# Last stage loaded at once, the last step's rows in one output product, Wo requested earlier, column-tiled softmax sums, and a new instruction order

## Chip, cores, metric

One core of a Trainium2 chip. The metric is the device time of one execution in microseconds (us); a kernel is judged by the median of its runs, and kernels are compared only with runs on the same chip. The time before was 1850.33 us, the median of 3 runs (1847.67 to 1852.43).

## The reference, cut to what matters

```python
def _A_ref(x, mem0, Wq, Wk, Wv, Wo, seg_len):        # x 1x2048x512, 32 heads of 128, segments of 32 rows
    mem = mem0                                       # 8 memory rows
    for s in range(n_seg):                           # 64 steps, one after the other
        h = concat([mem, x[segment s]])              # 40 rows
        q, k, v = h @ Wq, h @ Wk, h @ Wv
        p = softmax(where(mask, q @ k.T * scale, -1e9))
        o = (p @ v) @ Wo
        mem = o[:, :8]                               # the next step needs it
        outs.append(o[:, 8:])

def _B_ref(x, wqkv, wo):                             # linear attention, 32 heads of 16
    pq, pk = phi(q), phi(k)
    num = pq @ (pk.T @ v); den = pq @ sum(pk) + 1e-6
    return (num / den) @ wo

x = x + _A_ref(_layernorm(x), ...)                   # "layer 1"
x = x + _B_ref(_layernorm(x), ...)
x = x + _A_ref(_layernorm(x), ...)                   # "layer 2"
x = x + _B_ref(_layernorm(x), ...)                   # its output part is "the last stage"
```

Everything is bf16 at the interface. Only the memory rows tie a step to the one before; what depends on x alone (the "left" part: 32 queries and keys of a group of four steps for the first 8 rows of each segment) can be done ahead.

## The kernel before

The kernel records every operation with its reads, writes and an estimated cost, and a list scheduler puts them in one order per engine. A table OFFSET holds, for each kind of operation, how much earlier or later than its step it should be taken; the numbers were found by tuning. The parts that matter:

```python
# softmax sums of the x rows: ones-block matrix times the exponentials, in the full array
def sums(pe):
    o = tl.f32()[:, 256:512].rearrange("p (h q) -> p h q", h=8)
    pe.matmul(o, bo_sb[:, :], Px[:, :, :], start=True, stop=False)
    return pe.matmul(o[:, :, 0:8], bo_sb[:, :], PLL[:, g2, :, gl], start=False, stop=True)
# ... cut: projections, scores and output product run as four column tiles of 128x32 (tile_position=(0, 32 * j))

# scores of the left block, two halves; the keys and queries come from DMA transposes (step > 0)
turned(Wq_sb, "Wq", blk, bk, b, qTl[:, r2, hs, :, :], ("qTl", r2, b), False, step > 0)
turned(Wk_sb, "Wk", blk, bk, b, kTl[:, r2, hs, :, :], ("kTl", r2, b), False, step > 0)
at(step, "lefts")
for b in range(2):
    ...
    add("pe", mm, c_pe4(16, 32), reads=[("kTl", r2, b), ("qTl", r2, b)], tiles=[tl], mode="col")

# residual of a group: after the fourth step the left rows get an output product of their own
if g == 3:
    u = out_proj(oTl[:, :, :], [[("oTl", b)] for b in range(2)], False)
    add("pe", lambda pe: pick(pe, lambda d: sell_sb[:, d, :], u, False, True), ...)

# last stage: tile t in one of four buffer sets
(x, xk), (e, ek, rb, rk) = LAST[t % len(LAST)]
x_move(x, xs_view[t], ...); x_move(e, pq_view[t], ...)      # reload from DRAM
add("pe", md, ...)                                           # denominators into td
add("act", ... Ln ...); add("act", ... Exp scale=-1 ...)     # rb = 1 / den
add("dve", ... e = e * rb ...)
for c in range(4): add("pe", ... ty += e[:, c].T @ MB[c] ...)
add("dve", ... x = x + ty ...); x_move(o_view[t], x, ...)    # store
```

The softmax here doesn't subtract the row's maximum and nothing guards it: scores larger than these inputs give would overflow.

Of the kernel before, what the change touches and what calls it, by code (L numbers as in the profile page):

```python
# [19 lines left out]
MODE_SLACK = 13.61  # L20

LOOK = 0.082
# [3 lines left out]
    "ld0": (0.70,),  # L26
    "ld1": (-0.40,),
    "ld2": (2.30,),
    "ld3": (5.55,),
    "ld4": (8.15,),  # L30
    "startF": (-0.35,),
    "prepF": (4.00, -2.60, -0.45, 1.15, -4.65, 7.00, 14.55, -3.50, 0.90, -3.80, -3.10),
    "left0F": (-4.40, 2.85, 0.60, 32.60, -4.25, 0.00, 32.50, 0.00),
    "left1F": (0.05, -2.15, -4.10, 4.75, 3.10, 18.25, 7.20, 1.95),
    "leftv0F": (-3.10, -1.85),
    "leftv1F": (-1.40, -10.40),
    "leftsF": (-0.95, -0.75, 2.95, 0.45),
    "xlF": (-1.65,),
    "qk0F": (-10.50, -0.55, -0.25, 20.50, -0.40, -1.35, 3.25, -1.35),
    "qk1F": (-1.00, -1.60, 4.65, -4.45, -11.35, -1.55, 12.75, 1.30),  # L40
    "v0F": (7.00, 9.60),
    "v1F": (20.55, -10.50),
    "mem0F": (1.05, 7.85, -0.55, -5.55, -17.00, -0.80, -0.25, 0.65, 8.20),
    "mem1F": (2.70, -2.55, -1.85, 3.15, -3.55, -7.15, -0.35, -24.55, -0.75),
    "outF": (-1.20, 10.05, 1.30, 0.10),
    "nextF": (3.80, -27.25, 1.30),
    "xF": (3.05, -0.25, -1.40, 27.60, -0.70, -1.90, -2.30, -5.85, 1.30, 6.10, 1.25, 6.15, 2.10, -6.95, -10.55,
        -32.90, 1.90, 17.30, 22.35, 15.65, 14.45, 7.40, 2.20),
    "qk0": (-6.65, -8.45, 2.80, -2.85, 0.75, -1.95),
    "qk1": (0.10, 0.50, -3.40, 6.60, 0.30, 7.35, 4.45, 0.00),  # L50
    "v0": (-0.35, -1.85),
    "v1": (1.10, -1.15),
    "mem0": (-7.20, 3.30, -4.60, -15.00, -14.10, -29.60, -1.10, -8.65, 1.10),
    "mem1": (4.95, 4.35, 2.30, -3.40, 0.85, 0.30, -0.30, 0.55, -0.20),
    "out": (-5.75, 3.60, 2.10, 0.00),
    "next": (-2.35, -2.70, 4.60),
    "res": (46.85, 9.10, -4.95, 0.45, -2.55, -2.35, 3.70),
    "x": (-2.40, 4.35, 3.50, 2.50, -2.75, -1.05, 18.10, -12.50, 0.00, 2.95, -11.30, -1.85, -2.60, -8.75, 1.05,
        5.10, 2.15, 20.75, -0.75, -2.90, 22.45, 15.20, -6.80),
    "prep": (-2.95, 9.15, 2.55, 3.15, 5.35, 1.20, 8.00, 14.55, -3.30, -1.15, 2.05),  # L60
    "left0": (1.40, 1.75, -0.55, -3.10, 2.35, -0.10),
    "left1": (-1.30, -12.85, 2.90, 28.00, -8.10, 0.90),
    "leftv0": (33.85, -3.25),
    "leftv1": (8.30, -8.25),
    "lefts": (-13.05, 27.25, 3.50, 0.05),
    "xl": (3.95,),
    "bi": (3.50, 0.15, 0.85, 0.85, -1.40, -9.55, 1.30, -7.60, -0.40, -5.70, 7.90, 3.90, 15.75, -3.20, 9.80,
        -8.55, -3.95, 1.25, 19.45, -0.25, -5.15, -10.65, -5.50),
    "xL": (17.05, 17.65, -5.75, 4.55, 0.00, -4.45, -1.50, -0.10, -4.55, -3.55, -4.45, 2.55, 0.80, 6.30, -5.95,
        4.25, 6.20, -9.30, -0.65, 6.15, 11.35, -14.35, 0.00),  # L70
    "outL": (0.00, 4.55, 2.10, -7.75),
    "resL": (1.90, 17.60, -4.15, -8.15, -4.70, -0.80, 10.70),
    "biL": (0.00, 5.25, -8.20, 1.20, 5.75, 0.00, 6.85, 7.75, -3.55, 6.55, -0.45, 0.50, 0.40, 3.70, 10.65,
        -25.10, 17.00, -4.45, 1.45, -4.25, 10.90, -1.45, -0.20),
    "bm": (14.50, -2.55, -2.20, -1.25, -15.85, -11.15, -10.00, 0.00, -4.45, 11.90, 32.55, 2.50, -11.35),
    "boF": (-4.80, -11.80, 5.50, 2.35, -12.80, -4.45, -19.45, -9.45),
    "bo": (-31.10, 6.35, -4.05, 10.85, 22.70, 6.80, -2.55, -1.15),
    "boL": (2.25, 5.05, -6.15, 20.80, 7.70, -12.90, -0.15, -3.00, -9.15),
# [407 lines left out]
def _build_kernel(nc, A_x, A_mem0, A_Wq, A_Wk, A_Wv, A_Wo, A_seg_len, B_wqkv, B_wo, out):  # L486
# [6 lines left out]
    assert D == 512 and H == 32 and DH == 128 and M == 8 and SEG == 32 and S % 128 == 0  # L493
# [35 lines left out]
    sell_sb = sb("sell_sb", [128, 2, 128], F32R)  # L529
    outW = sb("outW_sb", [128, 3, 256], F32R)  # L530
# [44 lines left out]

    SCR = [("kTl", 1, 0), ("kTl", 1, 1)]
    scr_flat = kTl[:, 1, :, :, :].rearrange("p h j x -> p (h j x)")
    A8_sb = scr_flat[:, 0:128]
    scr_sb = scr_flat[:, 128:848]
    MEM0 = ("vl", 1, 0)  # L580
    mem0_sb = vleft[:, 1, 0:512]

# [10 lines left out]
    XV = ["xlnT", "vB"]  # L593

# [37 lines left out]
    for i, (W, v, nm, t) in enumerate(((Wq_sb, qk_view[0], "Wq", 12.4), (Wk_sb, qk_view[1], "Wk", 22.0),  # L632
                                       (Wv_sb, qk_view[2], "Wv", 31.0))):
        P.at(-9000 + 1000 * i, "ld%d" % (2 + i))
        late.append(add("act", lambda a, W=W, v=v: a.dma_start(W[:, :, :], v), 0.5, writes=[nm], dsem="d" + nm, lat=t))
    wo_view = A_Wo.rearrange("h e d -> e h d")
    P.at()
    for i in range(4):
        hs = slice(8 * i, 8 * i + 8)
        nd = add("sp", lambda s, hs=hs: s.dma_start(Wo_sb[:, hs, :], wo_view[:, hs, :]), 0.9, writes=[("Wo", i)],  # L640
                 dsem="dWo%d" % i, after=[late[-2]], lat=(12.4, 5.6, 5.7, 5.8)[i])
        late.append(nd)
    add("sp", lambda s: s.dma_start(wqkv_sb[:, :, :], B_wqkv.rearrange("(c p) f -> p c f", p=128)), 0.5,
        writes=["wqkv"], dsem="dwqkv", after=[late[-1]], lat=5.0)
# [38 lines left out]
    for j in range(4):  # L683
        q = slice(32 * j, 32 * j + 32)
        d = j % 2

        sel(scr_sb[q, 8 * d:8 * d + 8], ALU.not_equal, 1.0, 0, [[-1, 8]], 1, *SCR)

        o = 16 + 224 * d + 96
        sel(scr_sb[q, o:o + 24], ALU.not_equal, 1.0, -8, [[-1, 24]], 1, *SCR)  # L690

        for g4 in range(4):
            o = 464 + 128 * d + 32 * g4 + 24
            sel(scr_sb[q, o:o + 8], ALU.not_equal, 1.0, -8 * g4, [[-1, 8]], 1, *SCR)
# [5 lines left out]
    pool(lambda g: g.memset(A8_sb[:, :], 1.0), SCR)  # L700
    sel(A8_sb[0:8, :], GE, 0.0, 0, [[1, 128]], -16, *SCR)
    sel(A8_sb[0:8, :], GE, 0.0, 15, [[-1, 128]], 16, *SCR)
# [3 lines left out]
        reads=SCR, tiles=[tl])  # L706
# [40 lines left out]
    cnt = {"m": 0}  # L747

    def a_layer(base, first):
        def at(s, name):  # L750

            P.at(base + s, name + ("F" if s <= 0 else "L" if s >= NSEG or (s == NSEG - 1 and name == "x") else ""))
# [134 lines left out]
        def x_attention(s):  # L887
# [25 lines left out]
            def sums(pe):  # L913
                o = tl.f32()[:, 256:512].rearrange("p (h q) -> p h q", h=8)
                pe.matmul(o, bo_sb[:, :], Px[:, :, :], start=True, stop=False)
                return pe.matmul(o[:, :, 0:8], bo_sb[:, :], PLL[:, g2, :, gl], start=False, stop=True)
            add("pe", sums, c_pe(1, 256) + c_pe(1, 64), reads=["Px", ("PLL", g2), "bo"], tiles=[tl])
# [11 lines left out]
            for b in range(2):  # L929
# [13 lines left out]
                pvv = lambda pv=pv: pv.f32()[:, :].rearrange("p (n q) -> p n q", q=32)  # L943
                evac(oTb[:, s1, 16 * b:16 * b + 16, 8:32], lambda pvv=pvv: pvv()[:, :, 8:32], 384, tiles=[pv],
# [52 lines left out]

        def residual(G, g, w):
# [6 lines left out]
            def pick(pe, sel, u, first, last):  # L1005
                for d in range(2):
                    r = pe.matmul(tl.f32()[:, 256 * d:256 * d + 256], sel(d), outW[:, u, :], start=first and d == 0, stop=last,  # L1007
                                  skip_group_check=True)
                return r
            add("pe", lambda pe: pick(pe, lambda d: selx_sb[:, d, 96 - 32 * g:224 - 32 * g], w, g == 0, False),  # L1010
                0.42, reads=[("outW", w, 0), ("outW", w, 1), "selx"], tiles=[tl])
            if g == 3:
                u = out_proj(oTl[:, :, :], [[("oTl", b)] for b in range(2)], False)
                add("pe", lambda pe: pick(pe, lambda d: sell_sb[:, d, :], u, False, True),
                    0.42, reads=[("outW", u, 0), ("outW", u, 1), "sell"], tiles=[tl])
# [30 lines left out]
        for s in range(NSEG):  # L1046
# [6 lines left out]
            for b in range(2):  # L1053
                at(s, "qk%d" % b)
                hs = slice(4 * b, 4 * b + 4)
                turned(Wq_sb, "Wq", blk, bk, b, qT[:, r2, hs, :, :], ("qT", r2, b), True, QDMA[b] and s > 0)
                turned(Wk_sb, "Wk", blk, bk, b, kT[:, r2, hs, :, :], ("kT", r2, b), True, KDMA[b] and s > 0)
# [16 lines left out]
            if g == 2 and G + 1 < NT:  # L1074
                prepare(G + 1, s)
        w = out_block(NSEG)
# [74 lines left out]
    def b_mid(step, n):  # L1151
# [9 lines left out]
        for c in range(4):  # L1161
# [9 lines left out]
    LAST = [((x_sb[:, 0, :], ("x", 0)), OWN),  # L1171
            ((x_sb[:, 1, :], ("x", 1)),
             (half(qT[:, 0], 0), [("qT", 0, 0)], whole(kT[:, 0]), [("kT", 0, 0), ("kT", 0, 1)])),
            ((x_sb[:, 2, :], ("x", 2)),
             (half(qT[:, 0], 1), [("qT", 0, 1)], vimg[:, 0, :].bitcast(F32), [("v", 0, 0), ("v", 0, 1)])),
            ((vleft[:, 0, 0:512], ("vl", 0, 0)), LEFT)]

    def b_out(step, t, last):

        P.at(step, "boL" if last else "bo" if t else "boF")  # L1180
        k = t % len(LAST) if last else slot(t)
# [83 lines left out]
```

## Time and profile before

| | before |
|---|---|
| time, median | 1850.33 us |
| TensorE busy | 1760 us, 95% |
| start to the first next-memory product | 54.98 us |
| steps of both layers (62 between the first and last of 63 marks, twice), without the end of layer 1 | 1670.8 us |
| end of layer 1 (last next-memory product to the first of layer 2) | 58.05 us |
| last next-memory product of layer 2 to the first multiply of the last stage | 33.4 us |
| first multiply to last addition of the last stage | 30.5 us |

The marks are the starts of the last matmul that picks the next memory rows (L988 before, L1012 after) in a step, and of VectorE's first and last operation of the last stage.

### The profile page before, as it was taken

Reading aid. Unit: us, or ns where it says so; the run is one execution under the profiler, and the core shown is the slowest. Engines: PE = TensorE matmul, PEld = TensorE weight load, DVE = VectorE, ACT = ScalarE, POOL = GpSimd, SP = SyncE. Lnnn points to the kernel's source line nnn. Section 1 sums busy time; section 2 is a strip of 40 time slices with the busy share of each in tenths; the row PEclk is TensorE's granted clock in tenths of the full one; section 3 lists DMA queues with packets and bytes.
Section 4 is the critical chain, followed back from the end, with each engine's and each line's share of the span. In section 5 each row is a group of like instructions: output and inputs, shape, how many; then the busy total and the mean of one; then the engine's idle time right before and its main releaser. Section 6 shows DMA issues by size and latency. Waiting matters only on the chain.

```text
span 1850.0 us, 99018 instructions
## 1 busy us (share of the span) xinstructions
PE 1760.3 (95%) x45752; PEld 1181.3 (64%) x45861; DVE 1041.4 (56%) x3161; ACT 1207.3 (65%) x3133; POOL 74.7 (4%) x172
## 2 busy tenths in 40 slices
PE   5899999999999999999799999999999999999996
PEld 2566666666666666676456666666666676666662
DVE  3365555555555555555555555565655656555555
ACT  3566666666666676666466667666666766666655
POOL 3000000000000000000000000000000000000000
PEclk9999999999999999999899999999999999999998
DMA  9322222212121221222012122222221212223214
GB/s 358 92 42 38 39 40 36 45 38 46 37 42 37 38 44 40 43 38 40 22 26 40 38 46 41 46 43 38 43 41 38 49 40 43 41 41 55 43 34 125
DMA packets 221743, 95.53 MB, mean 52 GB/s; under 512 B 205096, under 2 KB 215472, under 8 KB 219792
## 3 DMA queue, kind: packets, MB, share of 16 engines
q1 hardware_dynamic: 214128, 61.01, 17.7%
q0 software_dynamic: 5616, 15.60, 3.0%
q10 hardware_dynamic: 1584, 12.58, 1.7%
q8 instruction: 358, 5.87, 1.3%
q14 instruction: 57, 0.47, 0.1%
HBM read 29.89 MB, written 10.49 MB: 22 GB/s over the span
## 4 chain that ended last, share of the span: by engine, by line
PE 84%; DMA 11%; ACT 2%; DVE 2%; issue 1%; ACTq 0%; SPq 0%; DVEq 0%
PE pb L764 38%; PE pb L963 16%; DMA arena_sb<-arena_sb 9%; PE pb L939 4%; PE pb L848 4%; PE pb L786 3%; PE pb L1007 3%; PE pb L865 2%; PE pb L1102 2%; PE pb L903 2%; ACT arena_sb L602 2%; PE pb L1138 1%; PE pb L879 1%; DMA Wk_sb<-in_A_Wk_dram 1%; PE pb L878 1%
## 5 line engine op out<-in xcount | busy, mean ns | idle before, releaser
L602 ACT ACTIVATE arena_sb<-pb 128x512 bf16<-128x512 f32 (+6 forms) x1369 | 704.7, 525 | 337.9 <-PE pb L764 269.7
L764 PE MATMUL pb<-Wk_sb,arena_sb 128*32 128x512 bf16 x5120 | 345.4, 381 | 4.8 <-DMA Wk_sb<-in_A_Wk_dram 4.6
L764 PE MATMUL pb<-Wq_sb,arena_sb 128*32 128x512 bf16 x5120 | 342.9, 383 | 4.7 <-DMA Wq_sb<-in_A_Wq_dram 0.6
L764 PE MATMUL pb<-Wv_sb,arena_sb 128*32 128x512 bf16 x5120 | 345.1, 379 | 0.3 <-issue 0.3
L963 PE MATMUL pb<-Wo_sb,arena_sb 128*32 128x256 bf16 x10368 | 324.2, 275 | 5.4 <-issue 3.0
L603 DVE CAST arena_sb<-pb 128x128 bf16<-128x128 f32 (+3 forms) x411 | 161.9, 394 | 246.0 <-PE pb L988 152.3
L963 PEld LDWEIGHTS pb<-Wo_sb,arena_sb 128*32 128x32 bf16 x10368 | 266.5, 97 | 28.2 <-DVE arena_sb L882 13.4
L924 DVE TENSOR_TENSOR arena_sb<-arena_sb 32x256 bf16<-32x256 bf16 x512 | 213.4, 417 | 108.1 <-ACT arena_sb L920 95.5
L603 DVE COPY arena_sb<-pb 128x512 bf16<-128x512 bf16 (+2 forms) x318 | 124.2, 391 | 175.0 <-PE pb L786 164.5
L764 PEld LDWEIGHTS pb<-Wk_sb,arena_sb 128*32 128x32 bf16 x5120 | 132.3, 97 | 128.4 <-DMA Wk_sb<-in_A_Wk_dram 4.8
L764 PEld LDWEIGHTS pb<-Wq_sb,arena_sb 128*32 128x32 bf16 x5120 | 120.8, 97 | 116.2 <-DVE arena_sb L1131 6.1
L602 ACT ACTIVATE outW_sb<-pb 128x128 fp32r<-128x128 f32 x287 | 79.8, 278 | 170.3 <-PE pb L963 139.1
L764 PEld LDWEIGHTS pb<-Wv_sb,arena_sb 128*32 128x32 bf16 x5120 | 130.9, 97 | 88.3 <-issue 1.6
L786 PEld LDWEIGHTS pb<-id_sb,arena_sb 128*32 128x32 bf16 x4288 | 75.5, 96 | 95.3 <-ACT arena_sb L602 61.9
L855 ACT ACTIVATE arena_sb<-pb 128x256 bf16<-128x256 f32 x252 | 96.5, 384 | 43.7 <-PE pb L848 35.2
L786 PE MATMUL pb<-id_sb,arena_sb 128*32 128x128 bf16 x4288 | 107.2, 221 | 16.6 <-ACT arena_sb L602 12.5
L926 DVE TENSOR_TENSOR arena_sb<-arena_sb 32x64 bf16<-32x64 bf16 x512 | 110.8, 216 | 14.9
L939 PE MATMUL pb<-arena_sb 128*128 128x128 bf16 x1024 | 114.5, 216 | 1.5 <-DVE arena_sb L926 1.5
L940 PE MATMUL pb<-arena_sb 128*128 128x32 bf16 x1024 | 106.3, 177 | 0.0
L848 PE MATMUL pb<-arena_sb 128*128 128x32 bf16 x2016 | 96.8, 178 | 7.4 <-DMA arena_sb<-arena_sb 7.2
L882 DVE TENSOR_TENSOR arena_sb<-pb,arena_sb 128x128 bf16<-128x128 f32 x252 | 72.7, 289 | 43.2 <-ACT arena_sb L870 24.2
L848 PEld LDWEIGHTS pb<-arena_sb 128*128 128x128 bf16 x2016 | 72.4, 96 | 27.9 <-DMA arena_sb<-arena_sb 9.4
(109 smaller groups left out, 2210.3 us busy)
## 6 DMA issues: line engine op xcount, KB each, us to landing
arena_sb<-arena_sb SPq DMA_TRANSPOSE x372, 2.7
Wq_sb<-in_A_Wq_dram ACTq DMA_DIRECT2D x1, 4096.0 KB, 13.5
Wk_sb<-in_A_Wk_dram ACTq DMA_DIRECT2D x1, 4096.0 KB, 24.5
Wv_sb<-in_A_Wv_dram ACTq DMA_DIRECT2D x1, 4096.0 KB, 34.8
Wo_sb<-in_A_Wo_dram SPq DMA_DIRECT2D x4, 1024.0 KB, 8.5
xs_scratch<-x_sb POOLq DMA_DIRECT2D x32, 128.0 KB, 2.6
pq_scratch<-arena_sb POOLq DMA_DIRECT2D x32, 128.0 KB, 2.7
x_sb<-xs_scratch POOLq DMA_DIRECT2D x16, 128.0 KB, 2.3
```

What stands on the lines that cost most here:

```text
L602: return e.activation(o() if callable(o) else o, i() if callable(i) else i, ACTF.Copy)
L603: return e.tensor_copy(o() if callable(o) else o, i() if callable(i) else i)
L764: r = pe.matmul(tl.f32()[32 * j:32 * j + 32, 0:512], blk[:, c, :], W[:, c, o:o + 512], start=(c == 0), stop=(c == 3), tile_position=(0, 32 ...
L786: r = pe.transpose(tt.bf16()[32 * j:32 * j + 32, 128 * i:128 * i + 128], img[:, k, o:o + 32], id_sb[:, :], tile_position=(0, 32 * j))
L848: r = pe.matmul(tl.f32()[:, o:o + 32], kk[:, hh, :, :].rearrange("p j x -> p (j x)"), qT[:, r2, hh, :, 0:8], start=True, stop=True)
L855: add("act", lambda a: a.activation(Pm[:, k, :, :].rearrange("p a q -> p (a q)"), tl.f32()[:, 0:256], ACTF.Exp, scale=SCALE), c_act(256), ...
L882: add("dve", lambda v: v.tensor_tensor(oTb[:, s % NO, 16 * b:16 * b + 16, 0:8], pv.f32()[:, 0:128].rearrange("p (n q) -> p n q", q=8), Rm[ ...
L924: add("dve", lambda v, q=q, j=j: v.tensor_tensor(Pbx[q, :, j, 0:32], Px[q, :, :], Rx[q, :, :], ALU.mult), c_dve(256) + 0.075, reads=["Px", ...
L926: add("dve", lambda v, q=q, j=j: v.tensor_tensor(Pbx[q, :, j, 32:40], PLL[q, g2, :, gl], Rx[q, :, 0:8], ALU.mult), c_dve(64) + 0.075, read ...
L939: pe.matmul(o, vimg[:, r2, e], Pbx[:, hh, :, 0:32], start=True, stop=False)
L940: return pe.matmul(o[:, :, 0:8], vleft[:, g2, e], Pbx[:, hh, :, 32:40], start=False, stop=True)
L963: r = pe.matmul(tl.f32()[32 * j:32 * j + 32, 0:256], oT[:, 4 * hh + n, :], Wo_sb[:, 8 * n + hh, 256 * d:256 * d + 256], start=(hh == 0 and ...
```

## The change

Its name speaks of the last stage. It has five parts: (1) the last stage's rows and queries come in eight large transfers into the room of the query weights, with room for each tile's reciprocals in the key weights; (2) the left rows of the last group lose the last step, which gets a selection of its own, so their output product no longer waits for it; the last step's images are transposed on TensorE; (3) Wo is requested in two pairs, behind Wk and behind Wv; (4) the softmax sums are column-tiled; (5) the whole OFFSET table and two scheduler constants are new. In the diff, "..." and the comments are mine, and it is cut to these parts.

```diff
-MODE_SLACK = 13.61
-LOOK = 0.082
+MODE_SLACK = 12.41
+LOOK = 0.074
 OFFSET = {                       # cut: every number of the table differs
@@ loads
-    dsem="dWo%d" % i, after=[late[-2]], lat=(12.4, 5.6, 5.7, 5.8)[i])
+    dsem="dWo%d" % i, after=[late[1 + i // 2]], lat=(12.5, 14.5, 7.3, 9.8)[i])
@@ sums
-    pe.matmul(o, bo_sb[:, :], Px[:, :, :], start=True, stop=False)
-    return pe.matmul(o[:, :, 0:8], bo_sb[:, :], PLL[:, g2, :, gl], start=False, stop=True)
+    for left in range(2):
+        for j in range(4):
+            q = slice(32 * j, 32 * j + 32)
+            o = tl.f32()[q, 256:512].rearrange("p (h q) -> p h q", h=8)
+            ...  pe.matmul(o, bo_sb[:, q], Px[:, :, :], ..., tile_position=(0, 32 * j))
+    add("pe", sums, ..., mode="col")
@@ residual
-    u = out_proj(oTl[:, :, :], [[("oTl", b)] for b in range(2)], False)
+    if G < NT - 1:
+        left_rows(G)             # the last group's product comes at step NSEG - 1, with a selection selz for its last step
@@ last step's images
-    turned(Wq_sb, ..., True, QDMA[b] and s > 0)
+    turned(Wq_sb, ..., True, QDMA[b] and 0 < s < NSEG - 1)
@@ last stage
-    (x, xk), (e, ek, rb, rk) = LAST[k]
+    rb, rk = RE[:, t, :].bitcast(F32), [("RE", t)]
+    if t < NT - 1:
+        e, ek, x, xk = XE[:, 0, t, :], [("XE", 0, t)], XE[:, 1, t, :], ("XE", 1, t)   # loaded 4 tiles at a time
```

## The prediction

> **What bounds the kernel now.** I read the page first, then the table of stretches, the timeline of TensorE in one period, the chain of waits at the two layer ends, and the groups of the last stage alone.
>
> ```profile
> PE 1760.3 (95%) x45752; PEld 1181.3 (64%) x45861; DVE 1041.4 (56%) x3161; ACT 1207.3 (65%) x3133; POOL 74.7 (4%) x172
> ...
> PEclk9999999999999999999899999999999999999998
> ```
>
> TensorE bounds nearly everything. The 64 steps of each of the two layers follow each other through the memory rows, and TensorE has work in every one. The table of stretches shows where that is not so:
>
> ```profile
> 20.00:40.00 20.00, 13.16 (x331) 6.71 (x320) 5.17 (x17) 6.30 (x13) 2.76 (x8) 0.83 0.93 360
> 40.00:60.00 20.00, 16.73 (x320) 9.16 (x322) 4.56 (x13) 9.09 (x22) 0.00 (x0) 0.91 0.91 242
> 200.00:400.00 200.00, 194.88 (x5250) 133.26 (x5257) 115.56 (x363) 135.28 (x355) 5.97 (x11) 1.00 0.23 40
> 1815.50:1848.00 32.50, 22.11 (x113) 9.34 (x116) 20.75 (x32) 20.23 (x33) 0.00 (x1) 0.89 0.53 164
> ```
>
> Columns are busy us of TensorE, weight loads, VectorE, ScalarE, GpSimd, then clock, DMA share and GB/s. There are four regimes. The start (0 to 70 us) waits for 16 MB of weights. The steady stretches (about 104 to 855 and 1000 to 1760) have TensorE busy 97%. The layer ends (about 890 to 925 and 1788 to 1815) are serial chains. The last stage (1815.5 to 1850) has no engine busy over 70%: it waits. Its groups:
>
> ```profile
> L1200 DVE TENSOR_TENSOR arena_sb<-arena_sb 128x512 bf16<-128x512 bf16 x16 | 10.8, 687 | 4.7 <-ACT arena_sb L1199 4.7
> L1199 ACT ACTIVATE arena_sb<-arena_sb 128x512 f32<-128x512 f32 x16 | 9.9, 632 | 0.4
> L1207 DVE TENSOR_TENSOR x_sb<-x_sb,pb 128x512 bf16<-128x512 bf16 x12 | 8.2, 686 | 5.9 <-PE pb L1204 5.8
> ...
> L1194 PEld LDWEIGHTS pb<-arena_sb 128*128 128x128 bf16 x52 | 3.4, 103 | 10.0 <-DMA arena_sb<-pq_scratch 9.5 <-issue 0.6
> ```
>
> The root is the last row: a tile's first product waits for its reload (9.5 us in all). Four buffer sets are recycled, so a reload is issued only when the tile four back is done with the buffer. VectorE's idle time, 4.7 + 5.8 + 1.2 us, is the echo of it.
>
> **What the Trainium skill says.** (1) "TensorEngine Tiling (Array Packing)", Tiling Modes, Key Properties: changing the tiling mode drains TensorE. The trace agrees: from the last projection matmul (4 column tiles) to the next start it is 206 ns in the same mode and 308 ns into a 128*128 product, so 0.10 us a switch. (2) "DMA: Bandwidth & Descriptors", Latency and other measured facts: about 2 us of fixed cost per transfer. The trace has 2.3 to 2.9 us for the 128 KB reloads, so eight large ones, issued early, should beat 32 small ones on the path. (3) "VectorE: DVE Perf Modes", Mode 1x: operands in f32 or PSUM give one result a cycle; [...]the rows above show 687 ns each (0.64 us from start to start back to back). (4) "TensorE: Matmul & The Clock Gate", Part 1: an idle TensorE falls to half clock. The trace shows 0.89 mean clock in the last stage.
>
> **Part 1, the last stage.** All rows and queries of 15 tiles come in eight transfers into the query weights' room once the last query projection is through (about 1788); tile 15 stays where it is; every tile has its own room for the reciprocals in the key weights. That is 3.9 MB with 27 us until 1815. At the 164 GB/s that this stage moves now it takes 24 us, at the start's 360 GB/s 11 us; the first tiles are there in either case. Removed: the reload waits. Left: VectorE 2 x 0.64 = 1.28 us a tile, ScalarE (0.69 + 0.63 less overlap) 1.23, TensorE 4 x 0.055 + 4 x 0.215 = 1.08. VectorE becomes the bound: 16 x 1.28 = 20.5 us from its first multiply. That stands at 1817.3 now, and the last addition ends at 1847.8, so 30.5 us become 20.5 plus about 1 us of gaps (PSUM holds four tiles in flight). The closing store is unchanged. **-9 us**.
>
> **Part 2, the layer ends.** The last step's memory rows go together with its other rows into one output product; the left rows of the three steps before it are projected in a product of their own that no longer waits for the last attention.
>
> ```profile
> 1797.98 0.50 ACT arena_sb L602
> 1798.48 0.04 issue
> 1798.52 3.71 PE pb L963 x128
> ...
> 1802.25 0.28 ACT outW_sb L602
> ```
>
> The chain holds two products of 64 matmuls in a row, 3.71 us; one of them (1.86) goes into the idle TensorE time of 1794 to 1797. The first layer's end shows 5.26 us for the same 128 at a lower clock, so 2.6. The DMA transposes of the last step: in the second layer the eviction of the second key image waits for a transpose to free its image buffer (ScalarE idle 1.67 us, TensorE 1.00), which goes; two more rounds of transposes on TensorE come in, 2 x 0.23 us. Net -0.8 there, +0.5 in the first layer, where the trace has no such wait. Together -1.86 - 2.6 - 0.8 + 0.5 = **-4.8 us**.
>
> **Part 3, the start.** The two first quarters of Wo are now requested once Wk is there, the other two once Wv is; before, the last two waited for the first two. The trace:
>
> ```profile
> 25.75 11.32 SPq L640 DMA_DIRECT2D Wo_sb<-in_A_Wo_dram  x2
> 37.16 1.30 SPq L777 DMA_TRANSPOSE arena_sb<-arena_sb  x1
> 38.56 4.29 SPq L640 DMA_DIRECT2D Wo_sb<-in_A_Wo_dram  x2
> ...
> 50.75 3.47 PE L963 MATMUL pb<-Wo_sb,arena_sb 128*32 128x256 bf16 x64 [2.83 <-issue]
> ```
>
> The last quarter lands at 50.66 and the first output product starts at 50.75. From 36 to 40 us the packets move only 166 GB/s against 420 before: a gap of about 1 MB, and smaller ones later. Filling them brings Wo to about 46; Wv, which shares with another MB, comes about 2.5 us later. TensorE idles 2.83 us there. **-3 us**.
>
> **Part 4, the steady state**, which the change's name leaves out: the softmax sums of the x rows (two 128*128 matmuls, 114 + 27 ns, 128 times) become eight column-tiled ones of the same streaming time, and all orders of instructions and two constants of the scheduler are tuned anew. I went through the order of all matmuls: from 104 to 855 us there are 126 full-array phases in 56 steps, 9 per 4 steps, 2 x 0.10 us each. In all 56 steps the sums stand in a small phase of their own kind, alone or with other small products. It is tempting to write 56 x 0.2 us a layer. But look where it stands:
>
> ```profile
> 469.14 0.23 PE L988 MATMUL pb<-selm_sb,outW_sb 128*32 128x16 f32 x8
> 469.20 0.40 PE L764 MATMUL pb<-Wv_sb,arena_sb 128*32 128x512 bf16 x4
> 469.46 0.78 ACT L602 ACTIVATE arena_sb<-pb 128x32 bf16<-128x32 f32 x2 [0.20 <-PE pb L988]
> 469.54 0.28 PE L915 MATMUL pb<-arena_sb,bo_sb 128*128 128x256 bf16 x1
> 469.65 0.19 PE L916 MATMUL pb<-arena_sb,bo_sb 128*128 128x64 bf16 x1
> 469.78 0.40 PE L764 MATMUL pb<-Wq_sb,arena_sb 128*32 128x512 bf16 x4
> ```
>
> L988 makes the next memory rows; L764 on Wq, the next step, needs them evicted. From the last L988 to that L764 it is never under 0.50 us over the 126 steps counted (0.26 to the eviction, 0.19 for it, 0.05 after), and 0.58, 0.67, 0.68 or 1.47 in the four steps of a period. The sums and their switches fill a wait that stays. Of the 0.87 us that a period loses there (interval less useful streaming, by the phases' own durations) I give a third back: 0.26 x 31 periods = **-8 us**, sums and new order together. This is the softest number.
>
> **Sum**: -9 - 4.8 - 3 - 8 = -25; 1850 - 25 = 1825 us.
>
> **Rivals.** (a) The switches are all saved, as the naive count says: 128 x 0.2 = 26 us instead of 8, hence about 1807. For it: TensorE is the bound at 97% and each switch is real time. Against: the 0.50 us wait behind it. (b) The steady state gives nothing, or the new order loses some us: DMA transposes and key evictions shift, and the waits of L786 for ScalarE (8.8 us in 104 to 855) grow. Then 1833 to 1840. For it: both kernels are tuned, and a new order is tuned to a model. (c) The last stage does not follow: the large reloads come late or the sequence PE, ScalarE, ScalarE, VectorE, PE, VectorE leaves bubbles, since all three engines stand at 1.1 to 1.3 us a tile. Then -4 instead of -9, 1830. Against: 27 us of lead, no shared buffers. (d) The start gains nothing, since Wv is later by what Wo is earlier: 1828.
>
> **Range and chances.** Last stage -6 to -11, layer ends -3 to -6, start 0 to -5, steady state +4 to -20: the last term is most of the width. Eight times in ten 1811 to 1838. Faster by over 2% means under 1813.3: it needs the steady state to give about 20 us instead of 8, 0.15. Slower by over 2% would need a steady state that loses over 50 us, 0.01. Within 2%: 0.84.
>
> **What would show it.** Last stage: VectorE busy over 90% between its first multiply and its last addition, some 21.5 us, and L1194 waiting for no DMA; wrong if DMA waits stay on it or it lasts over 25 us. Layer ends: 64 instead of 128 matmuls of L963 between the last attention and the residual addition. Start: the first output product before 48 us. Steady state: full phases per 4 steps below 9, but the interval from L988 to the next step's L764 not under 0.50 us; a period of 53.4 to 53.7 us shortened by about 0.3. The prediction fails if periods shorten by over 0.8 us (rival a) or lengthen (b).

## The result

The changed kernel took 1844.14 us (median of 4 runs, 1842.39 to 1846.36) beside 1851.28 us for the kernel before in the same session, a ratio of 0.9965 (95% interval 0.9947 to 0.9984). Two later series on other chips gave 0.9953 both. Here and below a ratio is the mean time of one kernel's runs over that of the other's of the same rounds, so not quite the ratio of the medians. So the change is worth 7 to 9 us, and not the 25 us predicted; it lies outside the range.

The two first profiles, by the marks above:

| stretch | before | after | change | predicted |
|---|---|---|---|---|
| start | 54.98 | 53.79 | -1.2 | -3 |
| steps without the end of layer 1 | 1670.8 | 1677.3 | **+6.4** | **-8** |
| end of layer 1 | 58.05 | 55.10 | -2.9 | -2.1 |
| end of layer 2 to the first multiply | 33.4 | 33.5 | +0.1 | -2.7 |
| first multiply to last addition | 30.5 | 21.2 | -9.3 | -9 |
| closing store | 2.1 | 2.2 | +0.1 | 0 |
| span | 1850.0 | 1843.1 | -6.9 | -25 |

One profile is one run, and runs differ by 3 us and more. Two further profiles of the changed kernel and one of the kernel before with only its last stage changed (same order until there) give for the second row 1676.6 and 1677.8 against 1674.7, so the loss in the steps is +4.5 us in the mean. Of this, 2.7 us lie in the first three steps (40.2 against 37.5 us), where what the start had gained is given back. From the fourth mark on the same five profiles give 1636.2, 1637.7 and 1637.2 us against 1632.6 and 1637.9: +1.8 us, less than the two profiles of the old order differ by. So the steady state proper gained nothing; that it lost is not resolved.

The page of the changed kernel:

```profile
PE 1758.4 (95%) x46693; PEld 1194.1 (65%) x46693; DVE 1017.6 (55%) x3168; ACT 1207.6 (66%) x3127; POOL 76.9 (4%) x182
...
PEclk8999999999999999999899999999999999999999
...
q8 instruction: 365, 5.98, 1.3%
```

By the page TensorE is busy as long as before (1758.4 and 1760.3 us), but the two pages are not alike: 109 matmuls (45861 weight loads, 45752 matmuls) left no record before, and none are missing here. A later profile of the same changed kernel (e9), which lacks 109 too, has 1742.8 us, and e3, with the old order and 108 missing, 1756.4. Like for like the new order has TensorE busy 14 to 17 us less, and from 100 to 1790 us idle 55.5 us (e9) instead of 42.7 and 46.0: what was saved in work came back as waits. The last line is the queue that brings the instructions themselves: 365 packets of 16384 bytes (358 before). It becomes important below.

**Last stage.** Its groups, by shape (columns as in the prediction: count, busy us, mean ns, then the idle time before and what ended it):

```profile
L1248 ACT ACTIVATE Wk_sb<-pb,eps_sb 128x512 f32<-128x512 f32 x16 | 10.6, 735 | 0.0
L1251 DVE TENSOR_TENSOR Wq_sb<-Wq_sb,Wk_sb 128x512 bf16<-128x512 bf16 x15 | 10.3, 685 | 2.4 <-ACT Wk_sb L1250 2.4
L1258 DVE TENSOR_TENSOR Wq_sb<-Wq_sb,pb 128x512 bf16<-128x512 bf16 x15 | 10.3, 685 | 0.0
...
L1245 PEld LDWEIGHTS pb<-Wq_sb,arena_sb 128*128 128x128 bf16 x60 | 3.9, 98 | 1.5 <-DVE arena_sb L1194 0.2
```

The weight load of a tile's first product (L1245) waited 9.5 us for reloads before and waits for none now; VectorE's additions have no idle time before them, its multiplies 2.4 us. VectorE is the bound, as predicted.

**Steady state.** One step in layer 2 of the changed kernel (TensorE and SyncE's queue, cut):

```profile
1306.35 0.23 PE L1012 MATMUL pb<-selm_sb,outW_sb 128*32 128x16 f32 x8
1306.40 0.29 PE L935 MATMUL pb<-arena_sb,bo_sb 128*32 128x256 bf16 x4
1306.51 0.21 PE L932 MATMUL pb<-arena_sb,bo_sb 128*32 128x64 bf16 x4
1306.57 0.26 PE L1012 MATMUL pb<-selm_sb,outW_sb 128*32 128x16 f32 x8
...
1307.20 4.66 SPq L790 DMA_TRANSPOSE arena_sb<-arena_sb  x3
...
1310.46 0.28 PE L827 MATMUL pb<-arena_sb 128*32 128x32 bf16 x16
1311.88 0.28 PE L827 MATMUL pb<-arena_sb 128*32 128x32 bf16 x16 [1.14 <-DMA arena_sb<-arena_sb]
```

Two things are to be seen. The sums (L935, L932) now stand between the two halves of the next-memory product (L1012), not behind it. And the two halves of the left scores (L827) follow each other directly, the second waiting 1.14 us for a DMA transpose. In the kernel before a projection of 16 and more matmuls stood between them, and there was no wait:

```profile
1309.96 0.27 PE L814 MATMUL pb<-arena_sb 128*32 128x32 bf16 x16
1310.06 0.39 PE L764 MATMUL pb<-Wv_sb,arena_sb 128*32 128x512 bf16 x4
1310.28 1.03 PE L764 MATMUL pb<-Wq_sb,arena_sb 128*32 128x512 bf16 x16
1311.14 0.27 PE L814 MATMUL pb<-arena_sb 128*32 128x32 bf16 x16
```

After the first 100 us the waits for a late transpose before the left scores sum to 11.9 us in this profile (9.5 and 10.6 in the two later ones of the same kernel) and to 0.1 us before. The full-array phases fall from 126 to 98 (104 to 855 us) and from 125 to 108 (1000 to 1760 us).

**Last step.** The output products of the changed kernel's last step:

```profile
1797.69 2.35 PE L987 MATMUL pb<-Wo_sb,arena_sb 128*32 128x256 bf16 x77 [1.81 <-issue]
1799.97 0.50 PE L1029 MATMUL pb<-outW_sb,selx_sb 128*128 128x256 f32 x2
1800.97 0.48 PE L1029 MATMUL pb<-outW_sb,sell_sb 128*128 128x256 f32 x2
1801.48 1.05 PE L987 MATMUL pb<-Wo_sb,arena_sb 128*32 128x256 bf16 x31
1804.45 1.14 PE L987 MATMUL pb<-Wo_sb,arena_sb 128*32 128x256 bf16 x33 [1.91 <-issue]
```

The last product has 64 matmuls instead of 128, as intended. But two products stop in their middle for 1.81 and 1.91 us, and "issue" means that nothing the profile shows was waited for. After the start all such stops of more than 0.25 us lie a multiple of 256 apart (within one) in TensorE's stream of instructions, and each ends 2.3 to 2.7 us after a packet of the instruction queue starts.

### The profile page after: what moved, and what is told of

It reads as the page before. It is cut to its first block, busy times and chain, and to the rows that moved or that the text cites. A ratio compares the mean times of both kernels' runs of the same rounds, so it can differ in the third digit from the quotient of the medians.

```text
span 1843.1 us, 100858 instructions
## 1 busy us (share of the span) xinstructions
PE 1758.4 (95%) x46693; PEld 1194.1 (65%) x46693; DVE 1017.6 (55%) x3168; ACT 1207.6 (66%) x3127; POOL 76.9 (4%) x182
## 4 chain that ended last, share of the span: by engine, by line
PE 83%; DMA 11%; ACT 3%; DVE 2%; issue 1%; ACTq 0%; DVEq 0%
PE pb L777 38%; PE pb L987 16%; DMA arena_sb<-arena_sb 9%; PE pb L959 3%; PE pb L861 3%; PE pb L1029 3%; PE pb L799 3%; PE pb L1137 3%; PE pb L916 2%; ACT arena_sb L608 2%; PE pb L878 2%; PE pb L1173 1%; DMA Wk_sb<-in_A_Wk_dram 1%; PE pb L892 1%; PE pb L891 1%
## 5 line engine op out<-in xcount | busy, mean ns | idle before, releaser
L608 ACT ACTIVATE arena_sb<-pb 128x512 bf16<-128x512 f32 (+6 forms) x1412 | 727.2, 523 | 359.8 <-PE pb L777 302.1
L777 PE MATMUL pb<-Wq_sb,arena_sb 128*32 128x512 bf16 x5120 | 357.5, 383 | 0.6 <-DMA Wq_sb<-in_A_Wq_dram 0.6
L777 PE MATMUL pb<-Wv_sb,arena_sb 128*32 128x512 bf16 x5120 | 356.9, 382 | 0.1
L609 DVE CAST arena_sb<-pb 128x128 bf16<-128x128 f32 (+3 forms) x334 | 118.5, 355 | 252.5 <-PE pb L1012 201.4
L609 DVE COPY arena_sb<-pb 128x512 bf16<-128x512 bf16 (+2 forms) x352 | 137.7, 392 | 204.5 <-PE pb L799 198.9
L777 PEld LDWEIGHTS pb<-Wk_sb,arena_sb 128*32 128x32 bf16 x5120 | 141.8, 97 | 126.1 <-DMA Wk_sb<-in_A_Wk_dram 5.3
L777 PEld LDWEIGHTS pb<-Wq_sb,arena_sb 128*32 128x32 bf16 x5120 | 133.4, 97 | 113.6 <-DVE arena_sb L609 24.2
L608 ACT ACTIVATE outW_sb<-pb 128x128 fp32r<-128x128 f32 x261 | 72.3, 277 | 114.4 <-PE pb L987 77.1
L799 PEld LDWEIGHTS pb<-id_sb,arena_sb 128*32 128x32 bf16 x4352 | 77.5, 97 | 90.8 <-ACT arena_sb L608 58.1
L959 PE MATMUL pb<-arena_sb 128*128 128x128 bf16 x1024 | 130.9, 217 | 0.0
L799 PE MATMUL pb<-id_sb,arena_sb 128*32 128x128 bf16 x4352 | 109.6, 221 | 14.7 <-ACT arena_sb L608 14.6
L960 PE MATMUL pb<-arena_sb 128*128 128x32 bf16 x1024 | 118.3, 177 | 0.0
L868 ACT ACTIVATE arena_sb<-pb 128x256 bf16<-128x256 f32 x252 | 96.1, 383 | 27.3 <-PE pb L861 20.6
L861 PE MATMUL pb<-arena_sb 128*128 128x32 bf16 x2016 | 97.0, 178 | 5.2 <-DMA arena_sb<-arena_sb 4.9
```

The source lines that it names most:

```text
L608: return e.activation(o() if callable(o) else o, i() if callable(i) else i, ACTF.Copy)
L609: return e.tensor_copy(o() if callable(o) else o, i() if callable(i) else i)
L777: r = pe.matmul(tl.f32()[32 * j:32 * j + 32, 0:512], blk[:, c, :], W[:, c, o:o + 512], start=(c == 0), stop=(c == 3), tile_position=(0, 32 ...
L799: r = pe.transpose(tt.bf16()[32 * j:32 * j + 32, 128 * i:128 * i + 128], img[:, k, o:o + 32], id_sb[:, :], tile_position=(0, 32 * j))
L861: r = pe.matmul(tl.f32()[:, o:o + 32], kk[:, hh, :, :].rearrange("p j x -> p (j x)"), qT[:, r2, hh, :, 0:8], start=True, stop=True)
L868: add("act", lambda a: a.activation(Pm[:, k, :, :].rearrange("p a q -> p (a q)"), tl.f32()[:, 0:256], ACTF.Exp, scale=SCALE), c_act(256), ...
```

## The experiments

My theory after the result: the gain of the steady state was taken back by the left scores, whose two halves the new order put back to back, so that the second waits for its transpose; and some more by instruction fetches that fall into dense runs of matmuls. The rivals: the sums' switches were worth nothing (my own prediction's reason for a small gain), or the parts of the change harm and only the new order saves it.

### e1: second half of the left scores later

```diff
     P.schedule()
+    def left_scores_later(n): ...     # cut
+    left_scores_later(9)
```

In the order that is already fixed, the second half of each left block's scores goes nine matmul groups later on TensorE, its Exp and its mask behind it (29 of 30 blocks; two groups in the first).

> The changed kernel with its order fixed; only the second half of each left block's scores (L827) goes nine matmul groups (about 2 us) later on TensorE, so that a transpose that lands late no longer stops it. Theory: the 14 us that these scores wait for a DMA transpose in the changed kernel's trace are on the path, so about 14 us go: 1830 us, ratio to before about 0.989. Rival 1: the wait only moves to the next reader of the same transposes or into the wait for the memory rows: 1841 to 1845 us. Rival 2: half of it comes back: about 1837.

1832.4 us against 1853.26 before, ratio 0.9888 [0.9872, 0.9904]. Of the waits before the left scores one of 0.5 us is left. (The 14 us of the expectation are the waits of the weight loads, 13.7; those of the matmuls are the 11.9 above.) The size was uncertain, since the changed kernel itself wasn't run on that chip (only e2, which is nearly it, 0.9971), so it was repeated as e10.

### e2: instruction boundaries moved

```diff
-        for c in range(4):            # four small transposes of the first memory
+        for c in [0, 1, 2, 3] * 16:   # the same, sixteen times: 60 transposes more
```

> The changed kernel with its order fixed and 60 tiny extra transposes of the first memory rows on TensorE in its idle time before 12 us (same result). Theory: the idle stretches of TensorE that the profile puts down to issue (8 after the start, 0.42 to 1.91 us, 7.9 us in sum, two of them in the last step with 1.81 and 1.91 us) are waits for the instruction stream at its 256-instruction boundaries; 120 more instructions move the boundaries, so these stand elsewhere or are gone, those of the last step too, and the time moves by -6 to +3 us although work was added. Rival: they are waits for data, in the last step for the large loads: then they stay at the same operations with the same lengths and the time is the same within 1 us.

1848.09 us, ratio 0.9971 [0.9954, 0.9988]. In its trace the stops sit at other places, those of 1.81 and 1.91 us are gone,

```profile
1797.82 3.46 PE L987 MATMUL pb<-Wo_sb,arena_sb 128*32 128x256 bf16 x119
1801.75 0.49 PE L987 MATMUL pb<-Wo_sb,arena_sb 128*32 128x256 bf16 x9 [0.48 <-issue]
```

and from the last next-memory product to the residual addition it is 17.17 us instead of 20.78 (19.57 before). So the stops hang on the position in the instruction stream and not on the work, and without them part 2 gives -2.4 us at the end of layer 2, near the predicted -2.7. The whole time did not fall, although all stops after the start sum to 4.1 us here and to 7.9 in the changed kernel; the steps took 1681.3 us, 4 more than the changed kernel's mean, and why is not shown.

### e3: the last stage alone

The kernel before with the eight large loads and the new buffers only (the diff's last part, and the OFFSET keys that it needs).

> The kernel before with the last stage alone changed (eight large reloads into the weights' room, own room for each tile's reciprocals). Theory: the last stage takes 21 us from its first multiply to its last addition in place of 30.5, so 1841 to 1843 us (ratio 0.995), and the steady state is the same to the microsecond. Rival: the loads meet the last step's DMA transposes, or hold up TensorE's instruction stream there, and give 2 to 4 us back: 1844 to 1846.

1848.05 us, ratio 0.9965 [0.9951, 0.9979], which is -6.5 us with an interval of -3.9 to -9.1. In its trace the first multiply to the last addition takes 20.8 us instead of 30.5. So the last stage alone accounts for as much as the whole change gains; all other parts together came to about nothing, within some 2 us.

### e4: the sums alone

The kernel before with the column-tiled sums (the diff's second part), scheduled anew with its own OFFSET numbers.

> The kernel before with the sums of the x rows in column tiles, scheduled anew with its own old numbers. Naive count: 2 switches of 0.10 us less at each of 128 sums: 1825 us. My theory: the sums stood in a wait that stays, so 1846 to 1851 us, with about 7 full-array phases a period in place of 9. Rival: the new list order makes new waits, at the left scores or elsewhere, and it is slower than before: 1852 to 1860.

1895.53 us, ratio 1.0222: 42 us slower. Neither the naive count nor my theory allowed for that; the rival had the sign. A mode change for one operation changes what the list scheduler takes next, and with numbers tuned to the old choice the second layer's order falls into stops like this one, seven times (20.1 us), where the attention to the memory rows waits for VectorE:

```profile
1062.59 0.21 PE L878 MATMUL pb<-arena_sb 128*128 128x32 bf16 x1 [2.87 <-DVE arena_sb L857]
```

The stops are only half of the loss. Between 1000 and 1800 us the granted clock falls to 0.5 at each of the seven, for 3.41 or 6.83 us, 37.5 us in sum, and nowhere else; in the kernel before it stays at 1.0 in that stretch. The 64 matmuls of the output product just behind this stop take 3.62 us instead of 1.86. TensorE is busy in 31.5 of the 37.5 us; half of that, about 16 us, is an estimate of what the clock took. With the stops this is about 36 of the 41 us that the second layer's steps lose (882.7 against 842.1 us).

### e5: the changed kernel again, for the second chip

> The changed kernel once more, unaltered, as the measure for the other kernels of this chip. Ratio to the kernel before as first measured, 0.9965, within 0.0025 either way: 1843 to 1851 us.

1846.88 us, ratio 0.9953 [0.9937, 0.9969].

### e6: the sums back in the full array, order unchanged

```diff
-    for left in range(2):
-        for j in range(4): ...            # eight column-tiled matmuls
+    pe.matmul(o, bo_sb[:, :], Px[:, :, :], start=True, stop=False)
+    return pe.matmul(o[:, :, 0:8], bo_sb[:, :], PLL[:, g2, :, gl], start=False, stop=True)
     add("pe", sums, ..., mode="col")      # the order is computed as for column tiles
```

> The changed kernel with its order fixed, only the softmax sums of the x rows as two full-array matmuls again, in the same places. In the trace of the changed kernel 132 of the places where sums stand have column-tiled neighbours on both sides, 64 of the 196 pieces have one full-array neighbour; pieces that are split round next-memory matmuls come twice, so about 64 of the 128 sums would make a full-array phase of their own. The naive count: 64 x 2 x 0.10 us = +13 us against the changed kernel of this chip (ratio about 0.9965 + 0.007 = 1.0035). My prediction's theory, that these switches lie in the 0.50 us wait from the last next-memory matmul to the next step's query projection: at most +4 us (ratio under 0.9990). If it is +13 or more, the sums' switches are worth their full price in this order, and the steady state lost the gain elsewhere (the left scores' waits).

1857.12 us, ratio 1.0011 [0.9998, 1.0024]. Against e5 on the same chip that is 0.0058 x 1854.7 = +10.8 us, near the naive count for the 64 sums and far from the 4 us of my prediction's theory. The trace says why. In the two steady stretches there are 27 and 29 more full-array phases (125 and 137 against 98 and 108), and they stand where they cost:

```profile
1318.46 0.23 PE L1005 MATMUL pb<-selm_sb,outW_sb 128*32 128x16 f32 x8
1318.63 0.28 PE L928 MATMUL pb<-arena_sb,bo_sb 128*128 128x256 bf16 x1
1318.74 0.19 PE L929 MATMUL pb<-arena_sb,bo_sb 128*128 128x64 bf16 x1
1318.87 0.26 PE L1005 MATMUL pb<-selm_sb,outW_sb 128*32 128x16 f32 x8
```

From the first half of the next-memory product to the second it is 0.41 us here and 0.22 us with column tiles (1306.35 to 1306.57 above): 0.19 us, ahead of the wait in which I had hidden them. Of 116 steps counted, 28 are of this kind. In another 28 the sums follow the last next-memory matmul with a projection behind them, and there the interval to the next step's query projection grows from 0.56 us (e5) to 0.80. In the other 60 the sums have a full-array product beside them or lie elsewhere, and the interval stays within 0.02 us. So 28 x 0.19 + 28 x 0.24 = 12.0 us by this count, 56 x 2 x 0.10 = 11.2 by the number of switches, and 10.8 were measured.

### e7: all parts with the old order numbers

The changed kernel with the OFFSET numbers and constants of the kernel before wherever a key exists in both.

> The changed kernel with all its parts, its instruction order computed with the order numbers and the two scheduler constants of the kernel before wherever a key is in both. If the loss in the steady state came with the parts themselves, this is no worse than the changed kernel (1845). If the order is fragile and the new numbers were needed to repair it, as the run with the sums alone in the kernel before showed (+42 us), it is about 1875 to 1895 us, with stalls of about 3 us in the second layer's attention to memory and the last stage still 9 us shorter than before.

1888.15 us, ratio 1.0175 [1.0160, 1.0190]: as e4, with the same kind of stops (seven, 20.0 us), each again with the clock at 0.5 for 3.41 or 6.83 us (27.3 us in sum). So the new numbers were not an extra gain on top of the parts; they were needed to undo what the sums do to the order.

### e8: the load of wqkv later

```diff
     left_scores_later(9)
+    wqkv_later(2)     # in the fixed order of SyncE: the load of wqkv behind the next two DMA transposes
```

The reason is in the start of the changed kernel: 1.5 MB of wqkv go out at 53.19, and the transposes behind them are late.

```profile
53.19 1.52 SPq L648 DMA_DIRECT2D arena_sb<-in_B_wqkv_dram  x1
...
62.95 0.62 PE L799 MATMUL pb<-id_sb,arena_sb 128*32 128x128 bf16 x16 [3.05 <-ACT arena_sb L608]
```

> The changed kernel with the second half of each left block's scores nine matmul groups later (as in the earlier run, ratio 0.9888), and besides the load of wqkv issued after the first two DMA transposes of step 1 instead of before them. Theory for the start: those transposes take 4 to 5 us because wqkv, 1.5 MB, is in flight with them, and TensorE waits 3.05 us at 62.95 for the eviction behind them; behind each other, that wait falls to about 1 us, the first steps end 2 us earlier, ratio about 0.9877. Rival: the wait comes from the order and not from the transfer, or the load hits the next step's transposes instead: ratio 0.9888 again, within the noise of 0.0016.

1840.06 us, ratio 0.9908 [0.9886, 0.9929]. Both were right in part: the wait of 3 us is gone, and another has come for the next step's transposes,

```profile
66.83 0.30 PE L827 MATMUL pb<-arena_sb 128*32 128x32 bf16 x16 [2.06 <-DMA arena_sb<-arena_sb]
```

so nothing is gained: the fourth next-memory product comes at 92.53 us, against 92.27 in e1 and 92.76 in e5. Moved behind them, the transfer is paid by the transposes of the next step. (In e7, where the old order numbers send it out at 46.5 us, the fourth product is the earliest of all, at 91.35: that the gain is lost hangs on the order too. No run tests this alone.) The profiles so far also show that the gain of part 3 was real up to the first next-memory product (52.4 to 53.8 us in seven profiles with the new start, 55.0 to 57.3 in three with the old one, so -3.3 in the mean) and mostly given back by the fourth step. No run has part 3 alone.

### e9 and e10: the changed kernel and e1 side by side

> The changed kernel unaltered, as the measure on this chip: ratio 0.9953 to 0.9965 to the kernel before; waits of TensorE for a late DMA transpose ahead of the second half of a left block's scores 9 to 12 us in sum, as in its two profiles so far (11.9 and 9.5).

> The second half of the left scores nine matmul groups later, the same kernel as in the first series, now beside the changed kernel on one chip. Theory: it takes away the 9 to 12 us of those waits and little comes in for them, so 7 to 12 us faster than the changed kernel of this series. The first series gave 15 us, but against a relative of the changed kernel; the run with wqkv moved as well gave 8. Rival: most of the wait only moves to the next thing that needs late transposes or ScalarE, under 4 us.

The changed kernel: 1845.54 us, ratio 0.9953 [0.9931, 0.9974], waits before the left scores 10.6 us. With the second half later: 1839.02 us, 0.9923 [0.9903, 0.9943], no such wait. The difference is 0.0030 x 1852 = 5.5 us, with a 95% interval of about 1 to 10 us: less than I expected and less than e1 seemed to say; e8 against e5 gives 8.4. The trace shows the transposed halves with other work between them (here the second half, broken by projection matmuls, with no wait before it), while the transposes themselves take no less time than before (three in 4.79 us, 4.66 above):

```profile
1302.49 4.79 SPq L790 DMA_TRANSPOSE arena_sb<-arena_sb  x3
...
1308.07 0.26 PE L827 MATMUL pb<-arena_sb 128*32 128x32 bf16 x13
```

Part of the 10 us goes elsewhere: the waits of TensorE's own transposes (L799) for ScalarE are 13.7 us instead of 9.5 in this pair of profiles, though they vary as much between profiles of one kernel (10.0, 13.7 and 9.5).

### e11: four groups instead of nine

```diff
-    left_scores_later(9)
+    left_scores_later(4)
```

> The same with four matmul groups instead of nine. The waits are 0.7 us in the mean and up to 1.4; one group of sixteen projection matmuls is 0.86 us. So four groups should already cover nearly all: waits under 2 us in sum and a time within 3 us of the version with nine. If the gain came from the moved Exp and mask on ScalarE and VectorE rather than from the late transpose, the two distances would differ more.

1839.92 us, ratio 0.9914 [0.9893, 0.9936], waits 0.7 us, 7.2 us faster than the changed kernel by the ratios. As expected: the two distances agree within the noise, so the distance need only cover the lateness of the transpose.

### e12: both

e10 with the 60 small transposes of e2.

> The version with nine groups and 60 tiny transposes more at the start, which shift every boundary of 256 instructions: in the first series this took 3.6 us out of the last step's output product on the changed kernel, while the whole time stayed (stalls of 0.3 to 1.0 us appeared elsewhere). Theory: the same here, so within 2 us of the version with nine groups, the stalls of 0.6 and 1.9 us in the last output product gone, others in their place. Rival: without the left waits the 3 us show in the time.

1838.05 us, ratio 0.9916 [0.9890, 0.9942]. The stops for instructions above 0.25 us add up to 3.6 us after the start instead of 7.5, yet one of 2.01 us remains in the last output product, and the gain, 1.3 us by the ratios, is not resolved. e10, e11 and e12 are the best versions of this series: 14 to 16 us under the kernel before and 5.5 to 7 under the changed one by their ratios, all within each other's intervals. (e1, the same kernel as e10, was 21 us under the kernel before on its chip, so the chips or series differ by some us.)

## Why the prediction was wrong

**Part 1, the last stage, was right**: predicted -9, measured -9.3 between the first multiply and the last addition, VectorE the bound (busy 93% of that stretch). The size fits in part by luck: back to back the operations stand 0.61 us apart, before and after, and not the 0.64 that I read, so 32 of them are 19.5 us, and the idle time between them is 1.5 us instead of 1. e3 shows it alone.

**Part 4, the steady state, failed: "0.26 x 31 periods = -8 us, sums and new order together".** The row shows +4.5 us; without the first three steps, which belong to the start, it is +1.8: no gain where 8 us were promised. Two of its claims fell.
- "The sums and their switches fill a wait that stays." That was read from the old order and carried over to a new one. The wait is still there (0.47 us at least from the last next-memory matmul to the next step's query projection), but in a quarter of the steps of the new order the sums stand ahead of it, and in another quarter it is too short to hold their switches. These are worth 10.8 us (e6), rival (a)'s full price for the half of the steps in which the sums would be phases of their own. Whether the claim held for the old order is not tested, since e4 changed the order with the sums.
- The new order was booked as part of the gain. It brought a wait that did not exist: 10.7 us in the mean before the second half of the left scores (e10 and e11 remove it and gain 5.5 and 7.2 us, e8 8.4 with wqkv moved as well). That was the mechanism of rival (b), "DMA transposes and key evictions shift", to which I gave only the end of the range. By my count of the traces 45 full-array phases less are worth 45 x 2 x 0.10 = -9.0 us; the left scores +10.7 by their waits, or +5.5 to +8.4 by what the runs gain without them; the stops for instructions +3.3 (3.8 us in the mean of three profiles against 0 and 1.1). With the runs' figure that makes -0.2 to +2.7 where +1.8 is measured. The first two are tested by runs; the third is read from traces only, and e12, made to test it, did not resolve it.

I also read the order as an independent part that could only help. e4 and e7 show that the parts and the order cannot be split: with the old numbers the sums alone lose 42 us and the whole change ends 32 us slower than the kernel before.

Two slips of the prediction did not matter: a third of the 0.87 us is 0.29, not 0.26, and the small reloads of the last stage took 1.9 to 3.2 us, not 2.3 to 2.9. Rival (b)'s other sign did not come: the waits of L786 for ScalarE from 104 to 855 us, 6.1 us by the trace and not 8.8, are 4.7 to 5.2 (L799) in the changed kernel's three profiles.

**Part 3, the start, was right at its mark and wrong in the sum.** The first next-memory product comes 3.3 us earlier in the mean, but the load of wqkv, which goes out only 1.4 us earlier (52.4 against 53.8 us in the mean, without e7 and e8), then meets the transposes of the first steps, and at the fourth mark it is 0.9 us (93.0 against 93.9, means of seven and three profiles). "Brings Wo to about 46" failed: the last quarter lands at 49.6 us in the mean of the seven, 51.5 in the three. So "the first output product before 48 us" was wrong too: it starts at 49.7 to 51.1, in the mean 1.6 us earlier. The other 1.6 us were luck: the 64 matmuls take 1.92 us with the granted clock at 1.0, instead of 3.47 with it at 0.5, which the prediction did not name.

**Part 2, the layer ends**: the first layer gave -2.9 (predicted -2.1). The second gave +0.1, because two instruction fetches fell into its products, 3.7 us on the path; e2 shows -2.4 for the same stretch without them. The mechanism was right; the loss came from a cost that I had not put in the sum at all.

In the sum, -25 became -7 to -9: about 10 us of the difference are Part 4, about 3 the end of layer 2, 2 to 3 the start with its first steps.

## What to carry to other kernels

A wait that hides a cost hides it only while the cost stands inside it: before counting it as hidden in a new order, ask where the instruction will stand. A retuned order is not a separate gain that can be added to the parts, and a new one should be searched for waits that the old did not have (here two readers of transposed images put back to back, cured by moving one four matmul groups later). An idle stretch of TensorE can cost more than its length: in e4 and e7 the granted clock fell with each stop. Before two profiles' busy times are compared, compare the counts of matmuls and weight loads. When a gain at one mark is gone at the next, look for the transfer that only moved.

## What the Trainium skill lacked or had wrong

- "Runtime: NRT & Kernel Launch", Instruction fetch mechanics, says that the fetch of the next block of 256 instructions is "hidden", and that crossing a boundary is "mostly hidden". The traces show TensorE stopped for 0.3 to 2.2 us at boundaries of 256 instructions, seven to nine times in a run of the changed kernel after the start, in runs of column-tiled matmuls; two such stops in the last step last 3.7 us. Why most of the 365 boundaries cost nothing, and why the kernel before has no stop of this length after the start, no run shows. The block size of 16 KB that this page and "Advanced Engine Details and Errata", ISA Cache, give agrees with the packets (16384 bytes, 365 for 93535 instructions of TensorE).
- "TensorEngine Tiling (Array Packing)", Key Properties, says that a mode change drains TensorE, without a size. Here it is 0.10 us a change; two matmuls in another mode within a column-tiled run cost 0.19 us (0.41 against 0.22 us), and 56 such phases measured 10.8 us.
- "DMA: Bandwidth & Descriptors", DMA Transpose (X-bar), has no latency of a small transpose from SBUF to SBUF. Here it is 2.5 us from issue to landing in the median of 368 and up to 5.2 us after the start (6.3 during it), and two issued 1.3 us apart behind 1.5 MB of another load hold TensorE up by 2.0 to 3.2 us in the profiles of the new order (1.2 us in the kernel before).
- No page tells that a trace can lack matmul records, and not in every profile of a kernel: the changed kernel's profile e9 lacks 109, the two others none. In the kernel before 39 of 104 of one group (L1102, 0.4 us each) are missing in 13 periods, which looks like idle time at each place; the page's two counts, 45752 matmuls and 45861 weight loads, show it.
